# Four slots for the first v tiles instead of two, and a third slot for banded scores

## The chip, the cores and the metric

The kernel runs on one core of one Trainium2 chip. The metric is the time of one execution in microseconds (us) on the device. Executions of one kernel in one call differ by up to 5 us here, and the median of the kernel before differs by up to 4.4 us from call to call, so a version is only compared with the kernel before in the same call. Every run lists the mean clock that TensorE was granted. All runs below count as the fast state. A mean clock of 0.997 and not 1.000 means 1.7 us more (3.4 us at half clock).

## The reference, cut to what matters

```python
def _A_ref(x, wqkv, wo):                       # S=2048, D=1024, 32 heads of 32
    qkv = (x @ wqkv) ...                       # q, k, v
    off = jnp.arange(8) * 2                    # each position looks at 8 earlier ones, 2 apart
    logits = einsum('bhsd,bhswd->bhsw', q, kg) * scale
    attn = softmax(where(mask, logits, -1e9))
    o = einsum('bhsw,bhswd->bhsd', attn, vg)
    return o.reshape(B, S, D) @ wo
# [cut] _B_ref: gelu(x @ w_in), layernorm of one half, w_sp over positions, product of the halves, @ w_out
g = sigmoid((x * gate_w).sum(-1))
return g * _A_ref(...) + (1 - g) * _B_ref(...)
```

## The kernel before

TensorE (PE) runs almost without a gap for the whole execution; the other engines and the DMA queue of SyncE work around it. Instructions are put in one fixed order for each engine when the kernel is built, from a model of the durations, so an engine that has to wait can't take up something else.

The attention works on eight groups of four heads. For a group, PE makes q and k (L292), then three blocks of banded scores (L354; four blocks in group 0) in four PSUM banks, where matmuls leave their results. ScalarE copies a block to a slot, a buffer in SBUF (L362; such a copy is called an eviction below), a DMA stores the slot to DRAM (`band_d`), another DMA loads it back in another layout (`att_L`), and VectorE makes the softmax and the products with v. The v tiles of the first three groups (L302) go the same way: ScalarE copies a tile to a slot (L304) and its last column, the gate's sum, to `gl_s` (L305); every four tiles a DMA stores a slot (`v_d`). Behind the last v tile stands a small matmul that needs all of `gl_s` (L404).

```python
band_slots = [reg(R_OFF + 30208 + 7 * BR * r, 7 * BR)... for r in range(2)]
band0 = reg(R_OFF + 34184, 2 * BR)...            # own slot for the small first block
vp_slots = [reg(R_OFF + o, 4 * VP)... for o in (36288, 37824)]
# [cut]
def vp_tile(i, bank=None, middle=None):
    # [cut] eight matmuls, L302
    st = vp_slots[(i // 4) % 2]
    nc.scalar.copy(st[:, i % 4, :]..., ps[:, 0:VP]...)        # L304
    nc.scalar.copy(gl_s[:, i:i + 1], ps[:, VP:VP + 1])        # L305
    if i % 4 == 3:
        for g in range(GP): sync.dma_start(dv, st[:, :, g * C:(g + 1) * C])
# [cut]
def band_blocks(g, first, step, n, pairs=None):
    if first == 0: st = band0
    else:
        st = band_slots[band_at[0] % 2]
        band_at[0] += 1
    # [cut] matmuls into banks 4 to 7, L354
    nc.scalar.copy(dst, src)                                   # L362
    # [cut] the stores of st to band_d[g]
# [cut]
for c in range(4):
    tiles = range(4 * c, 4 * c + 4) if c else ()
    for n, i in enumerate(tiles if c < 3 else ()):
        vp_tile(i, low_bank)
        if n == 0: first_bands(c - 1)
    if c == 1:
        for m in range(2): sync.dma_start(wvr[m], ...)         # two loads of 640 KB, needed much later
    # [cut] q and k of group 0
for i in tiles:
    vp_tile(i, low_bank)
    if i == 12: first_bands(3)
qk_tile(1, 0, 0)
gate_mm = nc.tensor.matmul(glT, gl_s[:], ident32[:], ...)      # L404
# [cut] the other half of v; the z2 products ("quads") of the MLP start at about 194 us and need VectorE:
def plus(out, a):                                              # L505
    last_add[0] = nc.vector.tensor_tensor(out[:, n], a[:, n], vs, ALU.add)
```

Of the kernel before, what the change touches and what calls it, by code (L numbers as in the profile page):

```python
# [11 lines left out]
F16 = mybir.dt.float16  # L12
# [7 lines left out]
HG = 4  # L20
# [13 lines left out]
BR = KW * HG  # L34
# [9 lines left out]
R_OFF = XS_OFF + 16384  # L44
# [3 lines left out]
VP = GP * C  # L48
# [5 lines left out]
def _sub_ap(t, offset_elems, dims):  # L54
    return bass.AP(tensor=t.tensor, offset=t.offset + offset_elems, ap=[list(t.ap[0])] + [list(d) for d in dims])
# [3 lines left out]
def kernel(  # L59
# [26 lines left out]
    def reg(off, n):  # L86
        return arena[:, off:off + n]
# [41 lines left out]
    v_slots_t = [reg(R_OFF + 12288 + 3840 * r, NJJ * C) for r in range(2)]  # L129
    qT_slots = [reg(R_OFF + 22016 + 2048 * r, 2048).rearrange("p (e n) -> p e n", e=2) for r in range(2)]  # L130
    kT_slots = [reg(R_OFF + 26112 + 2048 * r, 2048).rearrange("p (e n) -> p e n", e=2) for r in range(2)]
    band_slots = [reg(R_OFF + 30208 + 7 * BR * r, 7 * BR).bitcast(F16).rearrange("p (m k h) -> p m k h", m=7, h=HG) for r in range(2)]
    band0 = reg(R_OFF + 34184, 2 * BR).bitcast(F16).rearrange("p (m k h) -> p m k h", m=2, h=HG)
    nc.gpsimd.memset(band0[:, :, 0:W - 1, :], NEG)
    vst_slots = [reg(R_OFF + o, 2 * VR).rearrange("p (a c) -> p a c", a=2) for o in (19968, 34752, 36288, 37824)]
    vp_slots = [reg(R_OFF + o, 4 * VP).rearrange("p (i c) -> p i c", i=4) for o in (36288, 37824)]
    vq_slots = [reg(R_OFF + 39360 + 2 * VH * r, 2 * VH).bitcast(F32) for r in range(2)]
    vz_slots = [reg(R_OFF + 19968 + 2 * ZC * r, 2 * ZC).bitcast(F32) for r in range(2)]

# [97 lines left out]
    def pe(dur, ready=0.0):  # L237
        return take("PE", dur, ready)
# [8 lines left out]
    def act(dur, ready):  # L247
        if live[0]:
            advance(ready)
        return take("ACT", dur, ready)  # L250
# [6 lines left out]
    def dma(ready, dur, f, landed=None, timed=False):  # L257
        if not live[0]:
            return f()
        item = [ready, dur, f, landed, timed]  # L260
        due.append(item)
        return item

    def issue(item):
        if item in due:
            due.remove(item)
            ready, dur, f, landed, timed = item
            sp = take("SP", 0.62, max(ready, lanes[-8]))
            end = take("DMA", 1.2 * dur, sp + 0.6) + 1.1
            lanes.append(end)  # L270
            if timed:
                settle()
                behind, at = pinned[gate_act.ins.engine], len(nc.cur_bb.bb.instructions)
            f()
            if timed:
                for i in nc.cur_bb.bb.instructions[at:]:
                    tc.add_manual_dep(i, behind, SYNC, reason="not sooner")
            if landed is not None:
                landed(end)
# [17 lines left out]
    def vp_tile(i, bank=None, middle=None):  # L297
        ps = bank() if bank else banks[i % 2]
        for kt in range(KT):
            if kt == (2 if i else 6) and middle is not None:  # L300
                middle()
            nc.tensor.matmul(ps[:, 0:VP + 1], xT[:, kt, i * P:(i + 1) * P], wvp[:, kt, :], start=(kt == 0), stop=(kt == KT - 1))  # L302
        st = vp_slots[(i // 4) % 2]
        nc.scalar.copy(st[:, i % 4, :].rearrange("p (g d h) -> p g d h", g=GP, h=HG), ps[:, 0:VP].rearrange("p (g h d) -> p g d h", g=GP, h=HG))  # L304
        nc.scalar.copy(gl_s[:, i:i + 1], ps[:, VP:VP + 1])  # L305
        if i % 4 == 3:
            for g in range(GP):
                dv = bass.AP(tensor=v_d.tensor, offset=v_d.offset + (g * (S + 16) + 16 + (i - 3) * P) * C, ap=[[C, P], [P * C, 4], [1, C]])
                sync.dma_start(dv, st[:, :, g * C:(g + 1) * C])
# [16 lines left out]
    for i in range(4):  # L326
        vp_tile(i, middle=lambda: xpose(i + 1) if i < 3 else None)
    band_at = [0]
# [7 lines left out]
    def band_blocks(g, first, step, n, pairs=None):  # L336
        qt, kt_ = qT_slots[g % 2], kT_slots[g % 2]
        if first == 0:
            st = band0
        else:  # L340
            st = band_slots[band_at[0] % 2]
            band_at[0] += 1
        for item in stored.get(id(st), ()):
            issue(item)
        ready = pe(T_BAND * (0.3 if n < 3 else 1.0), band_free[0])
        lo = W - 1 if first == 0 else 0
        for m in range(n):
            e, b = divmod(first + m * step, 8) if pairs is None else (m // pairs, first + m % pairs)
            for q in range(2):
                skip = lo if q == 0 else 0  # L350
                at = P * b + QB * q
                for h in range(HG):
                    hp = slice(DH * h, DH * (h + 1))
                    nc.tensor.matmul(banks[4 + h][QB * q:QB * (q + 1), m * KW + skip:(m + 1) * KW], qt[hp, e, at:at + QB],  # L354
                                     kt_[hp, e, at - (W - 1) + skip:at + QB], start=True, stop=True,
                                     tile_position=(DH * h, QB * q), skip_group_check=True)
        band_free[0] = act(0.55 if n < 3 else 1.73, ready + 0.2) + 0.15
        if lo:
            nc.scalar.copy(st[QB:P, 0:n, 0:lo, :], _sub_ap(psum_all[QB:P, :], 4 * 512, [[KW, n], [1, lo], [512, HG]]))
        dst = st[:, 0:n, lo:KW, :]  # L360
        src = _sub_ap(psum_all, 4 * 512 + lo, [[KW, n], [1, KW - lo], [512, HG]])
        nc.scalar.copy(dst, src)  # L362
        bd = band_d[g]

        def landed(t):
            band_data[g] = max(band_data[g], t)

        stored[id(st)] = []
        for q in range(2):
            for e in range(1 if pairs is None else 2):  # L370
                k = n if pairs is None else pairs
                dst = bass.AP(tensor=bd.tensor, offset=bd.offset + (2 * first + 16 * e + q) * BS, ap=[[BR, QB], [2 * step * BS, k], [1, BR]])
                src = st[QB * q:QB * (q + 1), e * k:(e + 1) * k].rearrange("p m k h -> p m (k h)")
                stored[id(st)].append(dma(band_free[0], 0.1 * k, lambda dst=dst, src=src: sync.dma_start(dst, src), landed))

    def band_set(g, x):
        band_blocks(g, *BAND_SETS[x])

    def first_bands(c):
        band_blocks(0, *((0, 8, 2), (1, 1, 6, 3), (4, 1, 4, 2), (6, 1, 4, 2))[c])  # L380
# [5 lines that stand above are left out]
            if n == 0:  # L386
                first_bands(c - 1)
        if c == 1:
            for m in range(2):
                sync.dma_start(wvr[m], wq_v[:, :, 2 * D + VP + VH * m:2 * D + VP + VH * (m + 1)])  # L390
        if c == 2:
            load_wqk(2, sync.dma_start)
        for t in range(2):
            qk_tile(0, t, c)
            if c == 3 and t == 0:
                first_bands(2)
    for i in tiles:
        vp_tile(i, low_bank)
        if i == 12:
            first_bands(3)  # L400
# [569 lines left out]
    for n in range(0, len(quads), 2):  # L970
        p, i = quads[n]
# [400 lines left out]
```

## Time and profile before

| kernel before | |
|---|---|
| time | 666.96 us, median of 3 runs (666.34 to 667.82) |
| PE idle in the profiled span | 665.4 - 656.0 = 9.4 us |
| waits of PE that the list names | 5.4 us, of which 3.0 are the change's target |

PE's busy time on the page of the kernel before (columns: busy us, share of the span, instructions):

```profile
span 665.4 us, 10753 instructions
...
PE 656.0 (99%) x4194; PEld 316.1 (48%) x4194; DVE 451.5 (68%) x671; ACT 293.0 (44%) x621; POOL 6.6 (1%) x15
```

PE is busy 99% of the time, so a change to buffers can only win what PE still waits. That is in the list of waits on PE (who waited for whom: us in total, how often, the longest):

```profile
PE psum_all L354 <- ACT arena L362: 1.8, 2, 1.4
PE psum_all L292 <- ACT gl_s L305: 1.2, 1, 1.2
...
PE psum_all L434 <- DVE psum_all L505: 0.4, 2, 0.2
```

The timeline of the kernel before around the second of these waits (start us, duration us, engine, line, names and shapes; in brackets the idle time before it and what ended it):

```profile
27.91 4.09 PE L302 MATMUL psum_all<-arena 128*128 128x385 bf16 x24
...
32.63 0.48 ACT L304 CAST arena<-psum_all 128x384 bf16<-128x384 f32 x1 [5.85 <-DMA v_d<-arena]
...
33.06 1.60 ACT L362 CAST arena<-psum_all 128x1704 f16<-128x1704 f32 x1
33.22 2.95 PE L292 MATMUL psum_all<-arena 128*128 128x512 bf16 x12 [1.22 <-ACT gl_s L305]
```

ScalarE stands still for 5.85 us, until the store of v tiles 0 to 3 has landed and their slot may be written again. PE goes on with tiles 9 to 11 until its PSUM banks are full, then waits 1.22 us. The same view of the kernel before, for the two places where the change turned out to be decided; first around the gate matmul L404:

```profile
45.08 1.11 ACT L362 CAST arena<-psum_all 128x1136 f16<-128x1136 f32 x1 [2.28 <-DMA band_d<-arena]
...
47.30 0.23 ACT L305 COPY gl_s<-psum_all 128x1 f32<-128x1 f32 x1
...
48.13 0.39 PE L404 MATMUL psum_all<-ident,gl_s 128*16 128x128 f32 x2
```

The last score block of group 0 also waits (2.28 us) for a store. PE does not wait: the last gate copy ends at 47.30 + 0.23 = 47.53, and PE comes to L404 only at 48.13. The slack is 0.6 us. The list of waits on ScalarE of the kernel before, from 24 to 60 us:

```profile
ACT arena L304 <- DMA v_d<-arena: 5.9, 1, 5.9
ACT arena L362 <- DMA band_d<-arena: 2.3, 1, 2.3
```

Next, still in the timeline of the kernel before, the scores of group 5, the first wait of the list on PE:

```profile
160.82 1.82 ACT L362 CAST arena<-psum_all 128x1988 f16<-128x1988 f32 x1 [3.08 <-DMA band_d<-arena]
...
162.69 0.64 PE L354 MATMUL psum_all<-arena 32*64 32x71 bf16 x56 [1.43 <-ACT arena L362]
```

And the first add of the z2 quads:

```profile
195.73 4.49 DVE L707 TENSOR_TENSOR arena<-arena,att_A 128x4096 f16<-128x4096 bf16 x2
...
200.14 0.63 DVE L505 TENSOR_TENSOR psum_all<-psum_all,arena 128x448 f32<-128x448 f32 x1
...
200.82 2.43 PE L434 MATMUL psum_all<-arena 128*128 128x448 f16 x12 [0.21 <-DVE psum_all L505]
```

L505 stands behind two multiplies of 2.3 us in VectorE's queue and comes 0.21 us late for PE. How full VectorE is, in a table of busy times by stretch of the kernel before (the sixth to ninth value are VectorE, "DVE", and ScalarE, "ACT", with instruction counts in brackets):

```profile
core 0: us, PE busy (x) PEld busy (x) DVE busy (x) ACT busy (x) POOL busy (x), PEclk, DMA share, GB/s
164.00:200.00 36.00, 35.52 (x414) 17.36 (x413) 34.60 (x42) 25.93 (x39) 0.00 (x0) 1.00 0.68 160
200.00:240.00 40.00, 39.79 (x211) 20.44 (x209) 39.24 (x58) 29.17 (x83) 0.00 (x0) 1.00 0.28 75
```

VectorE is busy 34.60 of 36 us and then 39.24 of 40.

### The profile page before, as it was taken

The numbers are of one execution on the slowest core, as the hardware profiler recorded it, in microseconds if no ns is written. First come the engines' busy times: TensorE is split into PE (matmuls) and PEld (weight loads), VectorE is DVE, ScalarE is ACT, GpSimd is POOL, SyncE is SP. The second block draws the span as 40 slices with busy tenths as digits, with TensorE's granted clock in tenths as the row PEclk, the third lists the DMA queues.
The fourth block names the chain that finished last, engine by engine and source line by source line (L and its number), as shares of the span: only waits on it lengthen the run. The fifth ranks groups of instructions, "written<-read, shape, count | busy, mean of one in ns | idle before, by whom it ended". The sixth has DMA issues, their size and how long they took to land.

```text
span 665.4 us, 10753 instructions
## 1 busy us (share of the span) xinstructions
PE 656.0 (99%) x4194; PEld 316.1 (48%) x4194; DVE 451.5 (68%) x671; ACT 293.0 (44%) x621; POOL 6.6 (1%) x15
## 2 busy tenths in 40 slices
PE   8999999999999999999999999999999999999998
PEld 4544467444455555444444444444444444444444
DVE  1520789966999999998878666897679953333301
ACT  4354676555678677799654112121121122222221
POOL 1000000000000000001100000000000000000000
PEclk9999999999999999999999999999999999999999
DMA  9988555698486050248985568569745787543000
GB/s 214 185 207 227 121 114 136 156 242 184 102 219 181 1 146 9 64 126 207 277 223 177 115 163 170 124 191 290 96 123 147 165 189 195 120 97 98 32 33 33
DMA packets 229475, 98.16 MB, mean 148 GB/s; under 512 B 177440, under 2 KB 215728, under 8 KB 229424
## 3 DMA queue, kind: packets, MB, share of 16 engines
q1 hardware_dynamic: 229136, 97.27, 60.0%
q8 instruction: 33, 0.54, 0.4%
q10 hardware_dynamic: 288, 0.20, 0.1%
q14 instruction: 18, 0.15, 0.1%
HBM read 45.10 MB, written 36.61 MB: 123 GB/s over the span
## 4 chain that ended last, share of the span: by engine, by line
PE 86%; DVE 6%; SPq 4%; DMA 2%; issue 1%; ACT 0%; ACTq 0%; DVEq 0%
PE psum_all L434 73%; PE psum_all L292 11%; SPq L179 3%; DVE arena L707 2%; DMA band_d<-arena 1%; SPq L162 1%; DVE arena L711 1%; PE psum_all L354 1%; PE psum_all L302 1%; DMA v_d<-arena 1%; DVE arena L712 1%; SPq L190 1%; DMA att_L<-band_d 0%; PE psum_all L490 0%; DVE arena L716 0%
## 5 line engine op out<-in xcount | busy, mean ns | idle before, releaser
L434 PE MATMUL psum_all<-arena 128*128 128x512 bf16 (+5 forms) x2425 | 495.8, 367 | 0.5 <-DVE psum_all L505 0.4
L434 PEld LDWEIGHTS <-arena 128*128 128x128 f16 (+1 forms) x2425 | 237.1, 98 | 257.9 <-issue 1.7
L292 PE MATMUL psum_all<-arena 128*128 128x512 bf16 x512 | 115.0, 379 | 1.3 <-ACT gl_s L305 1.2
L292 PEld LDWEIGHTS <-arena 128*128 128x128 bf16 x512 | 48.4, 98 | 57.8 <-issue 2.0
L707 DVE TENSOR_TENSOR arena<-arena,att_A 128x2048 f16<-128x2048 bf16 (+1 forms) x44 | 73.4, 1704 | 0.3
L295 ACT CAST arena<-psum_all 128x512 bf16<-128x512 f32 x64 | 37.3, 588 | 46.0 <-PE psum_all L292 46.0
L580 DVE TENSOR_TENSOR arena<-arena 128x1024 f16<-128x1024 f16 (+3 forms) x31 | 18.8, 609 | 47.7 <-PE psum_all L434 35.7
L452 ACT COPY psum_all<-psum_all 128x512 f32<-128x512 f32 (+1 forms) x30 | 15.8, 527 | 77.5 <-PE psum_all L434 73.0
L814 ACT ACTIVATE arena<-psum_all 128x448 bf16<-128x448 f32 x64 | 34.2, 546 | 19.2 <-DVE psum_all L505 10.2
L1094 ACT ACTIVATE arena<-psum_all 128x512 bf16<-128x512 f32 x56 | 31.4, 600 | 20.9 <-PE psum_all L434 13.6
L582 DVE TENSOR_TENSOR arena<-arena 128x1024 f16<-128x1024 f16 (+3 forms) x31 | 18.7, 607 | 32.1 <-PE psum_all L434 19.0
L505 DVE TENSOR_TENSOR psum_all<-psum_all,arena 128x448 f32<-128x448 f32 (+1 forms) x58 | 37.0, 660 | 4.1 <-PE psum_all L434 3.4
L711 DVE TENSOR_TENSOR arena<-arena 128x2048 f16<-128x2048 f16 (+1 forms) x22 | 37.2, 1704 | 0.1
L362 ACT CAST arena<-psum_all 128x1988 f16<-128x1988 f32 (+3 forms) x25 | 34.0, 1358 | 7.2 <-DMA band_d<-arena 5.9
L476 ACT COPY psum_all<-psum_all 128x512 f32<-128x512 f32 (+2 forms) x30 | 15.6, 522 | 46.2 <-PE psum_all L434 45.2
L458 ACT COPY arena<-psum_all 128x512 f32<-128x512 f32 (+1 forms) x30 | 16.2, 544 | 36.3 <-PE psum_all L434 33.1
L463 ACT COPY psum_all<-psum_all 128x512 f32<-128x512 f32 (+1 forms) x30 | 15.9, 528 | 36.3 <-PE psum_all L434 35.5
L869 ACT ACTIVATE arena<-arena 128x896 bf16<-128x896 bf16 x32 | 30.5, 960 | 0.0
L581 DVE TENSOR_TENSOR arena<-arena 128x1024 f16<-128x1024 f16 (+3 forms) x31 | 18.4, 608 | 10.4 <-PE psum_all L434 10.3
L1296 DVE TENSOR_TENSOR arena<-psum_all,arena 128x512 bf16<-128x512 f32 x8 | 5.5, 691 | 29.3 <-ACT psum_all L476 29.3
L302 PE MATMUL psum_all<-arena 128*128 128x385 bf16 x128 | 22.6, 327 | 0.0
L576 DVE TENSOR_TENSOR arena<-arena 128x512 f16<-128x512 bf16 (+3 forms) x36 | 19.4, 569 | 2.8 <-DMA arena<-in_B_w_in_dram 1.5
(95 smaller groups left out, 402.5 us busy)
## 6 DMA issues: line engine op xcount, KB each, us to landing
arena<-v_d SPq DMA_DIRECT2D x8, 960.0 KB, 5.0
z_d<-arena SPq DMA_DIRECT2D x14, 512.0 KB, 4.3
arena<-z_d SPq DMA_DIRECT2D x14, 512.0 KB, 4.3
zg_d<-arena SPq DMA_DIRECT2D x56, 128.0 KB, 2.2
arena<-zg_d SPq DMA_DIRECT2D x32, 224.0 KB, 3.1
band_d<-arena SPq DMA_DIRECT2D x28, 248.5 KB, 4.6
arena<-in_A_wqkv_dram SPq DMA_DIRECT2D x16, 256.0 KB, 4.4
o_d<-arena SPq DMA_DIRECT2D x4, 1024.0 KB, 6.4
```

The lines of the kernel that those rows point to most:

```text
L179: chained(nc.sync.dma_start_transpose(xT[:, :, i * P:(i + 1) * P], x2[i * P:(i + 1) * P, :]))
L292: nc.tensor.matmul(ps[:], w[:, t, kt, :], xT[:, kt, 512 * c:512 * (c + 1)], start=(kt == 0), stop=(kt == KT - 1))
L295: nc.scalar.copy(dst[:, :, 256 * c:256 * (c + 1)], ps[:].rearrange("p (n e) -> p e n", e=2))
L302: nc.tensor.matmul(ps[:, 0:VP + 1], xT[:, kt, i * P:(i + 1) * P], wvp[:, kt, :], start=(kt == 0), stop=(kt == KT - 1))
L362: nc.scalar.copy(dst, src)
L434: nc.tensor.matmul(bank[:, 0:N], lhsT, rhs, start=(start and m == 0), stop=(m == n - 1), skip_group_check=True)
L505: last_add[0] = nc.vector.tensor_tensor(out[:, n], a[:, n], vs, ALU.add)
L707: lambda ws=ws, in0=in0, in1=in1: tt(p5[:, ws], in0[:, ws], in1[:, ws], ALU.mult)), False
L711: lambda a=p3[:, ws], b=p3[:, ws.start + 4:ws.stop + 4]: tt(a, a, b, ALU.add)), not n
L814: nc.scalar.activation(z2[:, i + 8 * a, ZC * c:ZC * (c + 1)], bank[:, 0:ZC], ACT.Gelu_apprx_tanh, accum_out=s1[:, 4 * n + c:4 * n + c + 1])
L869: return nc.scalar.activation(junk, src, ACT.Square, accum_out=(s2, s2h)[x][:, n:n + 1])
L1094: last_gelu[0] = nc.scalar.activation(z1s[:, f, a, :], bank[:], ACT.Gelu_apprx_tanh)
```

## The change

No work is added or removed. Each of the four groups of four v tiles gets a slot of its own, instead of two slots in turn, so that tile 8 needn't wait. The scores get a third slot, but only from group 1 on, because the place chosen for it (38848 and on) lies over the second v slot (37824 to 39360), which is in use during group 0.

```diff
-    band_slots = [reg(R_OFF + 30208 + 7 * BR * r, 7 * BR)... for r in range(2)]
+    band_slots = [reg(R_OFF + o, 7 * BR)... for o in (30208, 32196, 38848)]
-    vp_slots = [reg(R_OFF + o, 4 * VP)... for o in (36288, 37824)]
+    vp_slots = [reg(R_OFF + o, 4 * VP)... for o in (36288, 37824, 4096, 5632)]
@@ vp_tile
-        st = vp_slots[(i // 4) % 2]
+        st = vp_slots[i // 4]
@@ band_blocks
-            st = band_slots[band_at[0] % 2]
+            st = band_slots[band_at[0] % (3 if g else 2)]
```

More of the change, by code (lines that the diff above doesn't have):

```diff
@@ L131 @@
     kT_slots = [reg(R_OFF + 26112 + 2048 * r, 2048).rearrange("p (e n) -> p e n", e=2) for r in range(2)]
-    band_slots = [reg(R_OFF + 30208 + 7 * BR * r, 7 * BR).bitcast(F16).rearrange("p (m k h) -> p m k h", m=7, h=HG) for r in range(2)]
+    band_slots = [reg(R_OFF + o, 7 * BR).bitcast(F16).rearrange("p (m k h) -> p m k h", m=7, h=HG) for o in (30208, 32196, 38848)]
     band0 = reg(R_OFF + 34184, 2 * BR).bitcast(F16).rearrange("p (m k h) -> p m k h", m=2, h=HG)
@@ L135 @@
     vst_slots = [reg(R_OFF + o, 2 * VR).rearrange("p (a c) -> p a c", a=2) for o in (19968, 34752, 36288, 37824)]
-    vp_slots = [reg(R_OFF + o, 4 * VP).rearrange("p (i c) -> p i c", i=4) for o in (36288, 37824)]
+    vp_slots = [reg(R_OFF + o, 4 * VP).rearrange("p (i c) -> p i c", i=4) for o in (36288, 37824, 4096, 5632)]
     vq_slots = [reg(R_OFF + 39360 + 2 * VH * r, 2 * VH).bitcast(F32) for r in range(2)]
```

## The prediction

> **What bounds it now.** The page gives PE 656.0 us busy of a 665.4 us span at full granted clock: at most 9.4 us of idle PE can be had. The list of waits on PE names 5.4 us: 1.2 us of a q/k projection (L292) on ScalarE's gate copy (L305), 1.8 us of banded scores (L354) on their eviction (L362; the longer 1.4), 2.0 at the very start, 0.4 on a VectorE add (L505). The change aims at the first two.
>
> **What it changes.** No work is added or removed; two buffer rotations get longer.
> (a) v tiles: in the timeline the eviction of v tile 8 (L304) holds ScalarE idle 5.85 us, until 32.63, for the store of tiles 0 to 3 (issued 28.82, landed 32.53: 3.7 us), which frees slot 0. Five evictions pile up behind it; PE stands 1.22 us before 33.22, and the next projection tile comes 0.2 us late as well (1.94 us behind, not 1.73). With four slots nothing waits. [...] The chain of waits runs through this store, so about 1.4 us are on the critical path.
> (b) Scores: in head group 5 the 1988-column eviction (1.82 us) waits 3.1 us, until 160.82, for the store of group 4's block, and PE stands 1.43 us before 162.69. With a third slot this block takes one stored long before; the next takes the one that landed at 160.8, needed about 161.5. So this wait nearly goes. The 0.35 us before 191.91 (group 7) follows a gelu on ScalarE and stays.
>
> **How much lasts.** (a) comes where VectorE has slack (17.2 of 37 us busy from 50 to 87), and its later work is fed by transfers that follow PE's progress, so the whole later program should move up 1.4 us. (b) comes just before VectorE is full: 34.6 of 36 us from 164 to 200, 39.2 of 40 to 240. The chain of waits passes on VectorE from 164.55 (a score load landing at 164.50, behind a store issued at 154.5, which the third slot doesn't hasten) to 200.14, where L505 already releases PE 0.21 us late. PE that comes 1.4 us sooner will wait there longer instead. I expect at most 0.4 us of (b) to last.
>
> New hazard: the third slot lies over buffers of the v quads, first written near 88; its group-2 block, stored from 82.6 on, should land near 87. I expect no PE wait, but the margin is about 1 us.
>
> **Prediction.** 667.0 - 1.4 - 0.2 = 665.4 us; range 664.0 to 667.0. Faster by over 2%: 0.01; within 2%: 0.98; slower: 0.01.
>
> **What would show it.** (a) the 5.9 us L304 wait and the L292 wait on L305 gone, group-1 scores at 61.0 instead of 62.4. (b) no wait of L362 on a score store after 140; PE's wait on L362 falls from 1.8 to about 0.4, while its wait on L505 near 200 rises from 0.2 to about 1.5. If it stays 0.2, (b) lasted and the time is near 664.
>
> **What would make it wrong.** A new wait of the v quads' shared copy (L458) on a score store near 88; another order of stores and score loads on SyncE, which moves VectorE's chain by a microsecond either way; the loads between 150 and 162, where stores took 7 us to land, not moving up with PE.

## The result

After: 667.33 us median of 4 runs (666.85 to 667.44), before in the same rounds 667.24 us (666.34 to 667.82). The ratio is 1.0001, 95% interval 0.9984 to 1.0018: the same. Ratios here are the mean time of one kernel's fast runs over that of the other's of the same rounds, so not quite the ratio of the medians. Three more comparisons of the same two kernels (below) gave 1.0014, 1.0008 and 1.0010. All engines of the two kernels carry out the same instructions in the same order; only the waits differ.

PE's busy time on the page of the kernel after:

```profile
PE 652.1 (98%) x4136; PEld 316.7 (48%) x4194; DVE 451.3 (68%) x671; ACT 293.7 (44%) x621; POOL 6.6 (1%) x15
```

The 4 us less of PE mean nothing: 58 matmul records are missing (4136 for 4194). The weight loads are complete in both traces, so positions below are read from them. The list of waits on PE of the kernel after:

```profile
PE psum_all L434 <- DVE psum_all L505: 2.2, 2, 1.9
...
PE psum_all L404 <- ACT gl_s L305: 1.8, 1, 1.8
...
PE psum_all L354 <- ACT arena L362: 0.3, 1, 0.3
```

Against the list of before, both targets are gone or down to 0.3, and two others have come: 1.8 us at the gate matmul, and 2.2 instead of 0.4 us on L505. About three us won and three and a half lost (the table of positions below has 1.6 + 1.5 and 1.8 + 1.7) is the whole result; the views of after show where. The timeline of the kernel after, where v tile 8 waited:

```profile
27.50 0.48 ACT L304 CAST arena<-psum_all 128x384 bf16<-128x384 f32 x1 [0.72 <-PE psum_all L302]
...
31.83 4.48 PE L292 MATMUL psum_all<-arena 128*128 128x512 bf16 x19
```

The eviction of tile 8 starts as soon as its matmuls are done (27.50 instead of 32.63), and the projection starts at 31.83 instead of 33.22. Then, around the gate matmul:

```profile
45.81 1.11 ACT L362 CAST arena<-psum_all 128x1136 f16<-128x1136 f32 x1 [4.65 <-DMA band_d<-arena]
...
48.02 0.23 ACT L305 COPY gl_s<-psum_all 128x1 f32<-128x1 f32 x1
...
48.40 0.38 PE L404 MATMUL psum_all<-ident,gl_s 128*16 128x128 f32 x2 [1.79 <-ACT gl_s L305]
```

PE reaches the gate matmul 1.5 us sooner (48.40 - 1.79 = 46.61 instead of 48.13), but the last gate copy ends 0.7 us later than before (48.25 instead of 47.53). The list of waits on ScalarE of the kernel after, from 24 to 60 us, shows the one long wait that is left:

```profile
ACT arena L362 <- DMA band_d<-arena: 4.6, 1, 4.6
```

It was 2.3 us. The chain of waits of the kernel after names the store (start us, duration us, what):

```profile
41.66 3.61 DMA band_d<-arena
...
45.81 1.11 ACT arena L362
```

The store was issued at 41.66 and landed at 45.27. In the trace of before the same piece was issued at 41.75, and the store had landed by 44.9. So the store did not move, although its data were ready at 34.7 us before and at 29.6 after. What stands ahead of it is in the timeline of SyncE's queue of the kernel after (start us, time to issue):

```profile
34.78 3.25 SPq L190 DMA_DIRECT2D arena<-in_A_wqkv_dram  x3
38.12 4.15 SPq L190 DMA_DIRECT2D band_d<-arena  x4
```

The first of the three loads is one of the two of 640 KB; the other was issued at 31.27, ahead of three v stores. SyncE comes to the four pieces of the score store only at 38.12. The scores of group 5 in the timeline of the kernel after:

```profile
158.19 1.82 ACT L362 CAST arena<-psum_all 128x1988 f16<-128x1988 f32 x1 [0.18 <-PE psum_all L354]
...
161.45 0.65 PE L354 MATMUL psum_all<-arena 32*64 32x71 bf16 x56
```

The eviction waits 0.18 us instead of 3.08, and PE not at all. And the first add of the z2 quads:

```profile
196.18 4.49 DVE L707 TENSOR_TENSOR arena<-arena,att_A 128x4096 f16<-128x4096 bf16 x2
...
200.59 0.62 DVE L505 TENSOR_TENSOR psum_all<-psum_all,arena 128x448 f32<-128x448 f32 x1
...
201.26 2.05 PE L434 MATMUL psum_all<-arena 128*128 128x448 f16 x10 [1.94 <-DVE psum_all L505]
```

PE waits 1.94 us instead of 0.21. The busy times of the kernel after:

```profile
164.00:200.00 36.00, 34.51 (x407) 17.07 (x409) 34.22 (x42) 25.77 (x41) 0.00 (x0) 1.00 0.72 163
200.00:240.00 40.00, 38.74 (x205) 20.03 (x205) 39.26 (x57) 27.46 (x82) 0.00 (x0) 1.00 0.28 73
```

VectorE is as full as before (34.22 and 39.26 us; the columns are those of the table before).

A count by position says the same in one table. Both kernels have the same 4194 weight loads on PE in the same order. The table gives the start of some of them before, and by how much they start later (+) or sooner (-) in the profiles of the other kernels (worked out from the traces; the versions are explained below):

```
load no.   before   after  v_only band_only band3_all late_loads light_after
   200      27.69   -0.01   -0.19     -0.27     -0.12      +0.18       -0.11
   300      41.03   -1.59   -1.78     +0.21     -1.70      -1.41       -1.69
   400      54.51   +0.25   +0.63     +0.20     -1.71      -1.41       +2.09
  1400     148.45   +0.26   +0.64     +0.20     -1.70      -1.41       +2.10
  1600     167.16   -1.23   +0.45     -1.02     -3.20      -2.91       +0.60
  1900     191.02   -1.24   +0.44     -1.03     -3.21      -2.91       +0.59
  2000     200.82   +0.44   +0.25     +0.39     -1.68      -1.61       +0.18
  4000     622.25   +0.44   +0.25     +0.39     -1.66      -1.61       +0.10
```

Load 200 lies before the change can act: what stands there is a difference of the start. From there to load 300 every version with four v slots wins the same 1.6 us. In the kernel after, these 1.6 us are given back by load 400 (with 0.25 more), 1.5 us are won by load 1600, and given back by load 2000. After that nothing moves for 460 us.

### The profile page after: what moved, and what is told of

The parts are those of the page before. It is cut to its first block, busy times and chain, and to the rows that moved or that the text cites. A ratio compares the mean times of both kernels' runs of the same rounds, so it can differ in the third digit from the quotient of the medians.

```text
span 665.7 us, 10682 instructions
## 1 busy us (share of the span) xinstructions
PE 652.1 (98%) x4136; PEld 316.7 (48%) x4194; DVE 451.3 (68%) x671; ACT 293.7 (44%) x621; POOL 6.6 (1%) x15
## 4 chain that ended last, share of the span: by engine, by line
PE 88%; DVE 6%; DMA 3%; issue 1%; SPq 1%; ACT 1%; ACTq 0%; DVEq 0%
PE psum_all L434 72%; PE psum_all L292 11%; DVE arena L707 3%; PE psum_all L302 2%; DMA band_d<-arena 2%; SPq L190 1%; DVE arena L711 1%; PE psum_all L354 1%; DMA att_L<-band_d 1%; PE psum_all L317 1%; DMA arena<-in_B_w_in_dram 1%; DVE arena L712 0%; PE psum_all L490 0%; ACT arena L304 0%; DVE arena L716 0%
## 5 line engine op out<-in xcount | busy, mean ns | idle before, releaser
L434 PE MATMUL psum_all<-arena 128*128 128x512 f16 (+5 forms) x2391 | 493.9, 367 | 4.0 <-DVE psum_all L505 2.2
L292 PE MATMUL psum_all<-arena 128*128 128x512 bf16 x488 | 111.0, 379 | 2.6 <-issue 1.9
L707 DVE TENSOR_TENSOR arena<-arena,att_A 128x2048 f16<-128x2048 bf16 (+1 forms) x44 | 73.4, 1703 | 0.3
L505 DVE TENSOR_TENSOR psum_all<-psum_all,arena 128x448 f32<-128x448 f32 (+1 forms) x58 | 36.9, 658 | 4.1 <-PE psum_all L434 3.6
L362 ACT CAST arena<-psum_all 128x1988 f16<-128x1988 f32 (+3 forms) x25 | 33.9, 1356 | 6.3 <-DMA band_d<-arena 4.6
L458 ACT COPY arena<-psum_all 128x512 f32<-128x512 f32 (+1 forms) x30 | 16.2, 544 | 36.9 <-PE psum_all L434 33.1
L576 DVE TENSOR_TENSOR arena<-arena 128x512 f16<-128x512 bf16 (+3 forms) x36 | 19.3, 567 | 2.5 <-DMA arena<-in_B_w_in_dram 2.2
```

The source lines that it names most:

```text
L292: nc.tensor.matmul(ps[:], w[:, t, kt, :], xT[:, kt, 512 * c:512 * (c + 1)], start=(kt == 0), stop=(kt == KT - 1))
L434: nc.tensor.matmul(bank[:, 0:N], lhsT, rhs, start=(start and m == 0), stop=(m == n - 1), skip_group_check=True)
L576: return [lambda a=a: nc.vector.tensor_tensor(*a) for a in args]
L707: lambda ws=ws, in0=in0, in1=in1: tt(p5[:, ws], in0[:, ws], in1[:, ws], ALU.mult)), False
```

## The experiments

The theory (T) after reading the two traces: the v half's gain is given back at the gate matmul L404, because group 0 still has two score slots and the store that frees the first of them comes no sooner; the score half's gain is given back at L505, because VectorE is full there. The rivals: the new places of the slots cost something themselves; the full DMA engines set PE's pace by another road; VectorE's load has nothing to do with it. Fifteen versions were run, three of them the whole change again, in four calls, each call on one chip. "At 0.997" counts the runs with a mean clock of 0.997 or less.

| version | median us | before us | ratio, 95% interval | at 0.997 |
|---|---|---|---|---|
| v_only | 669.44 | 667.24 | 1.0026 (1.0005 to 1.0047) | 2 of 4 |
| band_only | 667.51 | 667.24 | 1.0015 (0.9989 to 1.0040) | 1 of 4 |
| band3_all | 665.50 | 667.24 | 0.9972 (0.9957 to 0.9986) | 0 of 6 |
| light_after (wrong result) | 667.59 | 667.24 | 0.9996 (0.9976 to 1.0016) | 3 of 4 |
| band3_first | 667.55 | 669.55 | 0.9975 (0.9953 to 0.9997) | 2 of 4 |
| after_again | 670.11 | 669.55 | 1.0014 (0.9994 to 1.0033) | 3 of 6 |
| light_band3_all (wrong result) | 664.62 | 669.55 | 0.9935 (0.9916 to 0.9953) | 0 of 4 |
| wz_15 | 667.72 | 669.55 | 0.9976 (0.9957 to 0.9994) | 4 of 6 |
| lag15 | 667.39 | 671.66 | 0.9931 (0.9912 to 0.9950) | 0 of 6 |
| band3_again | 667.21 | 671.66 | 0.9949 (0.9925 to 0.9973) | 2 of 6 |
| after_third | 671.96 | 671.66 | 1.0008 (0.9985 to 1.0031) | 5 of 6 |
| after_warm | 671.46 | 671.66 | 1.0000 (0.9982 to 1.0018) | 4 of 6 |
| late_loads | 665.68 | 667.23 | 0.9981 (0.9962 to 0.9999) | 1 of 6 |
| after_fill | 667.37 | 667.23 | 1.0006 (0.9987 to 1.0024) | 0 of 6 |
| after_fourth | 668.11 | 667.23 | 1.0010 (0.9991 to 1.0029) | 2 of 6 |

The kernel before showed 0.997 in none of its 11 runs of the first, second and fourth call, and in 7 of 11 of the third, in which it was slowest. Where it lost its clock there isn't known: no profile was taken of it in these calls.

### v_only: the v half alone

```diff
-            st = band_slots[band_at[0] % (3 if g else 2)]
+            st = band_slots[band_at[0] % 2]
```

> The v half of the change alone (four v slots, score slots two throughout). Theory T (the 1.5 us won at 33 us are given back when the last score block of group 0 waits for the store that frees score slot 0, because group 0 still has two score slots; PE then waits about 1.8 us at the gate matmul L404): the same picture as the whole change up to 62 us: no L292 wait near 33, a wait of 1.7 to 1.9 us of L404 near 48, group-1 scores at 62.4 to 62.8; then PE's 1.4 us wait on L362 in group 5 is back and the L505 wait near 200 is again about 0.2. Time 667.0 to 667.6. Rival R (the slots' new places or the third score slot cost something themselves, and v alone would keep its gain): 665.5 to 666.

The list of waits on PE of this version:

```profile
PE psum_all L404 <- ACT gl_s L305: 2.4, 1, 2.4
...
PE psum_all L354 <- ACT arena L362: 1.6, 2, 1.2
...
PE psum_all L434 <- DVE psum_all L505: 0.2, 1, 0.2
```

As T expected in kind: the gain of 1.78 us at load 300 is gone by load 400, in a wait of 2.4 us at L404, somewhat longer than expected (1.7 to 1.9). The longest wait on L362 is 1.2 us, the group 5 wait that the third score slot had removed, and the L505 wait is 0.2. The times missed the expectation: 667.3 in the profiled run, but 668.55 to 670.6 in the other three. Two of these ran at 0.997, and the third at 0.999. The v half keeps no gain of its own, so the rival in which the third score slot cost the gain falls. The slots' new places are still in this version; late_loads, below, speaks to them.

### band_only: the score half alone

```diff
-        st = vp_slots[i // 4]
+        st = vp_slots[(i // 4) % 2]
```

> The score half alone (third slot from group 1 on, v slots two). T: the L292 wait of 1.2 us near 33 is there, no L404 wait; no L362 wait in group 5, but PE waits 1.5 to 2 us on L505 near 200; time 667.0 to 667.5, so neither half gains alone. If VectorE is not what takes this half's gain back, the time is about 665.8 and the L505 wait stays 0.2.

The list of waits on PE of this version:

```profile
PE psum_all L434 <- DVE psum_all L505: 1.9, 2, 1.7
PE psum_all L292 <- ACT gl_s L305: 1.7, 1, 1.7
...
PE psum_all L354 <- ACT arena L362: 0.5, 2, 0.3
```

The wait at 33 us is back (1.7 us here), L404 is absent from the list, L362 is down to 0.3 at the longest, and L505 has 1.7 us. In the table of positions, 1.2 us are won between load 1400 and 1600, and 1.4 are lost between 1900 and 2000. The score half alone gains nothing, as expected.

### band3_all: a third score slot in group 0 as well

The v slots move to places that nothing uses yet at that time, which frees the third score slot's place for group 0.

```diff
-    vp_slots = [... for o in (36288, 37824, 4096, 5632)]
+    vp_slots = [... for o in (4096, 5632, 9216, 10752)]
-            st = band_slots[band_at[0] % (3 if g else 2)]
+            st = band_slots[band_at[0] % 3]
```

> The whole change, with the v slots moved off the third score slot's place, so that group 0 has three score slots too. T: the last score block of group 0 waits for nothing, L404 waits under 0.3 us, group-1 scores near 61.1 instead of 62.7, and if the transfers of the next 100 us follow PE, the whole program comes 1.5 us earlier: 665.5 to 666.0. Rival D (the full DMA engines between 20 and 44 us set PE's pace by another road): the L404 wait goes but an equal one appears before 62, time 667. Rival D2 (transfers around 140 to 164 don't follow PE): group-1 scores at 61.1 but the L505 wait near 200 grows from 1.9 to over 3 us, time 667.

The two waits over 0.2 us that are left on PE after the start and that have a named cause, from the list of this version:

```profile
PE psum_all L434 <- DVE psum_all L505: 2.0, 2, 1.8
...
PE psum_all L354 <- ACT arena L362: 0.3, 1, 0.3
```

There is no L404 wait, and the 1.7 us of load 300 are still there at load 4000. The time is 665.50 us (664.39 to 666.49), ratio 0.9972; a second time (band3_again, below), 0.9949. This is what the prediction had expected of the change. No equal wait appears before 62 us, so the rival in which the full DMA engines set PE's pace by another road falls. The L505 wait near 200 stays at 1.8 us: the score half is still lost, so the rival in which transfers don't follow PE (over 3 us at L505) is not seen here.

### band3_first: the third score slot in group 0 only

```diff
-            st = band_slots[band_at[0] % 3]
+            st = band_slots[band_at[0] % (2 if g else 3)]
```

> Four v slots (moved), a third score slot in group 0 only, two from group 1 on. T: the 1.7 us won by 41 us last, as in the version with three slots throughout (no L404 wait, weight loads 1.7 us ahead at 62 us); PE's 1.4 us wait on L362 in group 5 is back, the L505 wait near 200 only 0.2: the time equals that version's, 665.0 to 665.9, so a third score slot after group 0 is worth nothing by itself. If it were worth something, 666.5 or more.

The ratio is 0.9975, next to the 0.9972 of three slots throughout, but in another call (before: 669.55 us), so the absolute times of the expectation were missed. PE's longest wait on L362 was 1.8 us (1.4 expected), the L505 wait 0.2, as expected. In the profile the loads stand at -1.63 at load 1400 and, after the L362 wait and a stretch of half clock behind it, at +0.21 at load 4000; the clock records show that stretch from 162.4 to 165.8 us, which is 1.7 us, so without it the version would stand at -1.5. As far as these runs show, the third slot's whole worth lies in group 0, which is the one group that the change left out.

### late_loads: the same two score slots, but the store ahead of two loads

```diff
-        if c == 1:
+        if c == 2:
             for m in range(2):
-                sync.dma_start(wvr[m], ...)
+                # same loads, ordered behind the last store of group 0's first large score block
+                tc.add_manual_dep(sync.dma_start(wvr[m], ...).ins, stored[id(band_slots[0])][-1].ins.name, NOSYNC, ...)
```

> The whole change (two score slots in group 0), but the two 640 KB weight loads of the v quads are issued behind the store of group 0's first large score block, not ahead of it. Theory (the store is held up by the loads in front of it in SyncE's queue and on the full DMA engines): the store lands 3 us or more sooner, near 42 or before; ScalarE's wait of 4.6 us for it (L362 near 45.8) falls under 1.5 us, PE's wait at L404 under 0.3, and the time is 1.5 to 2 us under the whole change, the same as with three score slots. If the store lands near 45 all the same, something else holds it and the L404 wait stays.

The wait of ScalarE from 24 to 60 us for a score store, in the list of this version:

```profile
ACT arena L362 <- DMA band_d<-arena: 0.5, 1, 0.5
```

4.6 us became 0.5. The timeline of SyncE's queue of this version:

```profile
35.99 2.65 SPq L190 DMA_DIRECT2D band_d<-arena  x4
```

The store is issued from 35.99 on and its last piece lands at 41.74, 3.5 us sooner than in the kernel after. That piece was issued at 38.02 instead of 41.66 and took 3.7 us to land instead of 3.6: the gain lies in when SyncE issues the store, not in the transfer. Of the 3.6 us, 2.1 come from its sooner turn, and 1.5 from its first piece, which took 0.68 us to issue instead of 2.17 (why that one was slow isn't shown). L404 is no longer among PE's waits, the loads stand 1.4 us ahead at load 400 and 1.6 at 4000, and the time is 665.68 us, against 668.11 for the whole change and 667.23 for before on the same chip. The two score slots were never the limit by themselves: the store that frees the first was held up behind two loads that nobody needs until the v quads at 87 us. And the slots lie where the change put them, so the rival in which the new places cost the gain falls too.

### light_after: the whole change, one multiply less on VectorE

The result is wrong: one of group 3's multiplies with v (L707, 2.3 us, near 180 us) is left out.

```diff
-   lambda ...: tt(p5[:, ws], in0[:, ws], in1[:, ws], ALU.mult)
+   lambda ..., skip=(g == 3 and e == 1 and ws.start == 4): None if skip else tt(...)
```

> The whole change with one of VectorE's 2.2 us multiplies (L707, group 3) left out near 180 us; the result is wrong on purpose. T (the full VectorE takes the score half's gain back at L505 near 200): the L505 wait of 1.9 us falls to 0.3 or less, and the time falls by 1.6 to 2.2 us against the whole change, to 665.1 to 665.8. If VectorE's load is not what holds L505, the wait stays near 1.9 and the time within 0.5 us of 667.3.

From the list of waits on PE:

```profile
PE psum_all L404 <- ACT gl_s L305: 2.0, 1, 2.0
...
PE psum_all L434 <- DVE psum_all L505: 0.2, 1, 0.2
```

The L505 wait falls from 1.9 to 0.2 us, and between load 1900 and 2000 this version loses nothing where the change loses 1.7 us. That is the mechanism T expected. The time missed: 665.26 us in the one run at clock 1.000, but 667.2 to 668.3 in the three at 0.997. The profile is of one of those, and the busy times by stretch show why (the 1.00 or 0.50 ahead of the last two values is PE's granted clock):

```profile
core 0: us, PE busy (x) PEld busy (x) DVE busy (x) ACT busy (x) POOL busy (x), PEclk, DMA share, GB/s
45.00:49.40 4.40, 2.31 (x11) 0.92 (x11) 1.79 (x3) 3.20 (x9) 0.00 (x0) 1.00 0.61 135
49.40:52.80 3.40, 3.40 (x10) 1.22 (x9) 0.21 (x2) 0.59 (x1) 0.00 (x0) 0.50 0.72 165
```

After the 2.0 us wait at L404 the clock is at half for 3.4 us. The clock records give 49.37 to 52.79, so 3.41 us, and half of that, 1.7 us, is lost. This explains why the version stands at +2.09 at load 400, and not at +0.4.

### light_band3_all: three slots throughout, the same multiply left out

> Three score slots throughout and four v slots (moved), with the one 2.2 us multiply of VectorE left out (wrong result on purpose). T: no L404 wait and no L505 wait over 0.3 us; both halves of the change last: 1.7 plus 1.5 us under the kernel before, 663.6 to 664.4. If VectorE does not take the score half back, it stays near 665.5.

664.62 us where before has 669.55, ratio 0.9935; no run at 0.997. The loads stand at -2.75 at load 1900 and at -3.02 at load 2000, so nothing is lost at the first L505; by load 2100 they stand at -2.16, mostly in two later waits on L505 of 0.5 and 0.15 us. The L505 wait was above the expected 0.3, and the time 0.2 us above the expected range. About 0.9 of the score half's 1.5 us last (the version stood at -1.24 before it). So VectorE is what takes that half back, and taking 2.3 us of work from it at one place gives only part of it.

### wz_15: VectorE's sums moved into its idle time

On top of band3_all, the weights of the first z2 half are loaded every 1.5 us instead of every 3, so that VectorE can make their sums (L576, 4.2 us) before 153 us, when it is idle, and not at 158.

```diff
-            load_later(0, clock["PE"] + 6.0, 3.0)
+            load_later(0, clock["PE"] + 5.0, 1.5)
```

> Three score slots throughout, and the weights of the first z2 half loaded every 1.5 us from 5 us behind the v quads on instead of every 3 us from 6 on, so that VectorE makes their sums (4.2 us) in the 7 us in which it stands idle before 153, not at 158. T: VectorE reaches L505 near 200 about 1.5 us or more sooner, PE's wait there falls under 0.5, and the time is 663.6 to 664.6. If the loads, closer together, delay the score stores of group 3 and the v load near 130, new PE or VectorE waits show there and the gain is lost.

A miss. The sums moved to 143.7 to 148 us, but the L505 wait is still 1.8 us. The score load that VectorE needs next landed at 155.3 us instead of 150.4 in band3_all (152.8 in the kernel after), behind the closer loads, and VectorE was idle for 7.4 us again, only later. The backlog starts with the score load that lands near 163 us, and that did not move (162.9 us, 162.8 in band3_all). Four of the six runs were at 0.997; the other two took 665.9 and 666.4 us.

### lag15: L505 before the second multiply

On top of band3_all, nothing is added or left out; the modelled time at which VectorE's queue is filled is set back by 1.5 us where the z2 quads begin, so that the two L505 adds stand before the second 2.3 us multiply.

```diff
     def advance(t):
-        settle()
+        t -= lag[0]; settle()          # lag[0] is 1.5 in the first steps of the first two quads
```

> Three score slots throughout and four v slots (moved), and VectorE's order changed where the z2 quads begin: the first two adds (L505) stand before the second 2.3 us multiply (L707), not behind it; no work added or taken. T (the place of L505 in VectorE's queue is what takes the score half's gain back): PE's wait of 1.8 us on L505 near 200 falls under 0.5, both halves last: 1.2 to 1.6 us under the version with three slots alone, about 3 us under the kernel before; mean clock 1.000 in all runs[...]. Rival: VectorE is full from 164 to 240 us and hands the time back at a later L505 (PE waits of L505 sum to 1.5 us or more between 200 and 275): no gain over three slots alone.

Run beside it on the same chip:

> Three score slots throughout and four v slots (moved), again, beside the others on one chip: 1.5 to 2 us under the kernel before; L505 wait near 200 of 1.8 us; if a PE wait of that length can drop the clock, some of the runs show 0.997 and 1.7 us more.

667.39 us against 667.21 without the reordering: no gain. (By the mean lag15 is 1.0 us lower, but two of the six runs of band3_again were at 0.997 and none of lag15's; the medians of the runs above 0.997 are 667.39 and 666.90.) My theory in the narrow form (the place of one add in the queue) falls, and its rival stands. The waits on PE of lag15:

```profile
PE psum_all L434 <- DVE psum_all L505: 2.4, 2, 1.5
...
PE psum_all L434 <- ACT psum_all L517: 0.7, 1, 0.7
```

Three us of waits remain, now spread: 0.8 and 0.7 us between 190 and 275 us, 1.5 us behind 275. On this chip band3_again has one of 3.0 us at L505. VectorE hands the time back at another place. band3_again itself confirms band3_all (ratio 0.9949), with two of six runs at 0.997, as its expectation allowed; its L505 wait of 3.0 us missed the expected 1.8, and by the medians it is 4.5 us under before, where 1.5 to 2 were expected.

### The clock: after_again, after_third, after_warm, after_fill, after_fourth

> The whole change as it stands, again, beside the kernel before on one chip. T: L404 waits 1.7 to 2.4 us near 48, and in executions where the PE clock falls to half for 3.4 us after that wait (mean clock 0.997 instead of 1.000, as the profile of the run with the lighter VectorE showed from 49.4 to 52.8 us), the time is 1.7 us longer: some runs near 667.3, some near 669. The kernel before, whose wait near 33 is 1.2 us, should show it less often. If the clock has nothing to do with that wait, before and after show the lower clock equally often.

> The whole change, a third time: as the kernel before within 0.5 us in the runs at clock 1.000, 1.7 us above in those at 0.997; about a third to a half of the runs at 0.997.

> The whole change with four dummy matmuls (0.86 us) ahead of the gate matmul L404, so that PE's wait near 47 is broken up; results stay right. T (a PE wait of about 2 us there can halve the clock for 3.4 us): the longest wait near 47 falls to about 1.2 us or less, gate matmul about as late as in the whole change, no half-clock stretch near 50 us in the profile and fewer runs at 0.997 than the whole change; time about that of the whole change at clock 1.000. If the clock falls anyway, the cause of the drop is another.

> The whole change with eight dummy matmuls (1.7 us) ahead of the last projection tile before the gate matmul, so that PE computes where it waited; results stay right. Theory (a PE wait of about 2 us can halve the clock): no half-clock stretch near 50 us, fewer runs below clock 1.000 than the whole change beside it, the remaining ones from the L505 wait near 200; L404 wait under 0.5; time as the whole change at clock 1.000, within 0.5 us. If the clock falls as often as in the whole change, the waits near 47 are not its cause.

> The whole change again, for the comparison of clocks and of times on the same chip: L404 wait 1.5 to 2.4 us, clock under 1.000 in a third of the runs or more; time as the kernel before within 1 us.

The whole change is within noise of before in three more calls (ratios 1.0014, 1.0008, 1.0010). In 10 of these 18 runs the clock was at 0.997 or less. after_again's profile has the half clock from 50.6 to 54.0 us, behind an L404 wait of 2.2 us; after_third's has it for 6.8 us from 201.1 on, where PE had waited 3.2 us at L505. Its expectation (half of the runs) was missed upwards: five of six. after_fourth's L404 wait of 2.8 us lay above the expected 1.5 to 2.4.

after_warm told nothing: its dummies needed a PSUM bank that was not free, so a wait of 1.6 us stayed in front of them, and with after_third's clock falling near 201 us and not near 50, there was nothing to compare.

after_fill puts the dummies where their bank is free:

```diff
+    fill_bank = low_bank(); half_bank[0] -= 1   # the next tile's own bank, overwritten by it
+    [nc.tensor.matmul(fill_bank, xT[:, 0, 0:P], xT[:, 0, 0:512], ...) for _ in range(8)]
     qk_tile(1, 0, 0)
```

The L404 wait is 0.5 us instead of 2.8 in after_fourth on the same chip, none of six runs is at 0.997 instead of two, and the time is 667.37 us instead of 668.11, though PE has 1.7 us more to compute. That agrees with the theory that the wait can drop the clock. Six runs against six are too few to call it shown for this place, all the more as the L505 wait also differed (0.7 instead of 2.0 us at the longest). And the kernel before, which has no L404 wait in its profile, was at 0.997 in 7 of 11 runs of the third call: that wait can hardly be the only way to lose the clock.

Why some waits cost the clock and others don't can be read from the traces. In all 16 profiles that hold clock records, every change of the clock comes a whole number of stretches of 3.413 us after the first record, so the stretches of each execution are known. Where the clock fell during the work, PE had stood idle within the one stretch before it (no matmul and no weight load, gaps over 0.1 us) for 2.02 us in light_after, 2.17 in after_again and in after_third, 1.91 in band3_first and all 3.41 in after_warm. A longer wait that falls on two stretches did not do it: v_only's 2.4 us are 0.81 and 1.52, band3_again's 3.0 us are 1.73 and 1.26. Nor did 1.78 us in one stretch in band3_all, or 1.89 in the kernel after. In these profiles the line is near 1.9 us of one stretch; it isn't sharp, as after_again has 1.92 near 201 us without a fall.

## Why the prediction was wrong

The prediction was 665.4 us, range 664.0 to 667.0; measured were 667.3, the same as before.

- (a), the first wait: right. The L304 wait of 5.9 us and PE's wait at 33 us are gone, and PE is 1.6 us ahead at load 300 (predicted 1.4).
- "So the whole later program should move up 1.4 us": this is the step that failed. Group-1 scores, its sign, came at 62.6 us and not at 61.0. The argument was that VectorE has slack there and that transfers follow PE's progress. The slack of VectorE was beside the point, and one transfer did not follow. The last score block of group 0 waits for a store that lands at about 45 us in both traces (44.9 and 45.3), though PE is 1.6 us sooner in one, because it stands behind two weight loads in SyncE's queue. That wait was in the profile of before, 2.28 us of ScalarE at 45.08, and it cost nothing there because PE came 0.6 us after the last gate copy. The prediction leaves it out. With PE 1.5 us sooner and the gate copies 0.7 us later, 1.5 + 0.7 - 0.6 = 1.6 us of wait are to be expected; the profile has 1.79. band3_all and late_loads remove it in two different ways and both get the predicted time within 0.3 us (665.50 and 665.68 us).
- (b), the scores of group 5: right. The 3.1 us eviction wait fell to 0.2, PE's wait on L362 from 1.8 to 0.3.
- "PE will wait there longer instead": right, and slightly short. The L505 wait near 200 is 1.9 us (predicted about 1.5). Of (b), nothing lasted, where I allowed 0.2 us in the sum. light_after shows that VectorE's load holds L505.
- The new hazard over the v quads' buffers did not come: the list of waits has no L458, and the loads between 600 and 1400 keep their distance.
- What would make it wrong was listed in three points, and none of them was the cause.

What stays open: how much of the spread of up to three microseconds in the runs at clock 1.000, and of the 4.4 us between calls, comes from waits of the same kind. In the two slower calls the gains over before are larger than the positions show: light_band3_all is 4.9 us under before by the medians, where its positions, against the one profile of before, give 2.2. The profiles are of one execution each, and none was taken of the kernel before in the slower calls.

## What to carry to other kernels

A wait that costs nothing in the profile is a limit with a slack, and the slack is worth reading off before the gain upstream of it is counted: here 0.6 us stood behind a gain of 1.5. When a buffer is deepened, ask of every slot whether its release follows the engine that is sped up, or a queue that is not; and look whether the one phase that is excepted from the deeper rotation, here group 0, is the phase that needs it. The cheapest cure was not another buffer but the order of the queue: two loads with 40 us to spare stood ahead of a store that PE was waiting for.

## What the Trainium skill lacked or had wrong

- "TensorE: Matmul & The Clock Gate", section "What's actually happening", has PE at half rate after at least one idle window of about 3.4 us, the windows running free of the kernel. The half rate and the length agree with the traces (clock 0.50 for 3.413 us). What it takes differs: stretches of half clock followed PE waits of 2.0 (light_after), 2.2 (after_again) and 1.8 us (band3_first), well under a window, and in some executions only: the profiles of v_only (2.4 us), band3_again (3.0 us) and band3_all (1.8 us) have waits as long and no such stretch. The section "HAM oscillation — how this bites in real kernels" gives idle gaps over about 3.4 us as the rule to keep; here a gap of 2 us could cost 1.7 us more. What the page lacks is how much idle time within one window is enough: about 1.9 of 3.41 us in these profiles, and how a wait falls on the windows decides (see the clock above).
- "DMA: Bandwidth & Descriptors", section "Anatomy of one DMA", puts a fixed cost of about 2 us on a DMA, for the path through GpSimd; the stores here go through SyncE's queue, for which that section gives no figure. A 106.5 KB piece of the score store took 3.6 us from issue to landing (41.66 to 45.27), and, the larger part here, up to 12 us from the data being ready to the issue (29.6 to 41.66), waiting in SyncE's order. That second time is no part of the page's sum, and the runs showed that it is the one to look for.
- "Perfetto Trace Analysis", section "Optimization Strategy", says to find the gaps of the engine that matters and the semaphore behind each. It has nothing on waits that are hidden and become gaps once another is closed: 2.28 us of ScalarE that cost PE nothing before, 4.65 us that cost PE 1.79 after.
